# List scheduling carried on through the last two chunks, the routing, the first weight split and the gathering

## The chip, the cores and the metric

One core of one Trainium2 chip. The metric is device time in microseconds (us) of one execution of the whole program. The engines are TensorE (PE, matmuls; PEld its weight loads), VectorE (DVE), ScalarE (ACT), GpSimd (POOL) and SyncE (SP, which here only starts DMAs). Each engine works through its own list of instructions in order.

## The reference

A recurrence over 768 steps for 4 batches x 8 heads with a 40x40 state, and then a mixture of experts on its 3072 output rows (320 wide, 8 experts, inner width 1024):

```python
for t in range(S):
    y[:, :, t] = einsum('bhd,bhde->bhe', r[:, :, t], state)
    Sa = einsum('bhde,bhe->bhd', state, a[:, :, t])
    state = state*w[:, :, t][:, :, None, :] - einsum('bhd,bhe->bhde', Sa, b[:, :, t])
    state = state + einsum('bhd,bhe->bhde', v[:, :, t], k[:, :, t])
x = y.transpose(0, 2, 1, 3).reshape(3072, 320)
do_compute = x @ w_skip > 0; xc = x[do_compute]; logits = xc @ w_gate
out = x; out[do_compute] = xc + softmax(logits).max(1) * (relu(xc @ w1[e]) @ w2[e])   # e = argmax(logits)
```

## The kernel before

**The recurrence** runs in NC=24 chunks of 32 steps, in 6 phases of 4 chunks. The 32 (batch, head) pairs are handled in two halves w=0 and w=1. Decays and triangular systems (32x32 inverses, on DVE) are prepared per pair of chunks and for the next phase; they depend on the inputs alone. What depends on the chunk before is a chain, which runs once for each chunk c and half w:

- `rs` (PE `pc<-rrt,SS`, odd chunks' end): the decayed state goes into the operand tile R1;
- `ux` (PE `pc<-R1t,L1t`, then one ACT copy to UX), `uq` (PE `pc<-UX,TB`, then four ACT copies `R1t<-pc`);
- two mask multiplies on the corner of R1 (`R1t<-R1t,mc 64x256`, POOL; DVE in chunk 23);
- `sst` (PE `ps<-R1t,L2t`, two groups, 104 columns in an even chunk, 72 in an odd one, 32 in the last): from its result ACT (even chunks) or DVE (odd chunks) copies the state into the R1 of the next chunk, and DVE forms YT, the chunk's output, transposed;
- in odd chunks `pc<-L2t,R1t`, whose copy SS feeds the next `rs`.

When both halves of a chunk are done, `yt` (PE `pc<-mc,YT`) turns YT round, the rows go to XS and by DMA to out, and `pq<-wx,YT` gives the scores. `route` picks each token's expert: DVE, a small rank matmul `pq<-oh,mc` on PE, more DVE, and an indirect DMA `xg<-XS,ix` that POOL starts and that collects the rows of each expert in memory. In the table below a chunk is bounded by the start of its DMA `out<-XS`.

**The end.** The rows of the first expert are loaded ahead (`ex`), and the tokens of the last two chunks are added by one-hot matmuls: `xacc` (`pc<-mc,ex`) and two `xadd` (`pc<-ex,XS`, for chunks 22 and 23). Meanwhile split(0) has turned the first expert's raw weights WR into a rounded top part WH and a rest WL = WR - WH, each 128x5632. Then `l1` of expert 0 begins (`px<-xH,WH`); all eight experts follow, and out rows are written by scatter DMAs.

**What sets the order.** Class Rec records instructions as tasks with their reads and writes. plan() is a list scheduler with a table of costs per engine (cost()), a priority (keys(): place in the program less the length of the path behind it), and the PSUM banks: want() gives a task that opens a new tile a bank of its group when it starts, PC+PQ (`pc_101` to `pc_103`, `pq_100`) or PS (`ps_104`, `ps_105`); `px_106` and `px_107` are given by hand. flush() then emits each engine's instructions in the order of the planned starts. What is recorded appears in the profile as L255, what is emitted directly, in the order of the program text, as L129. In this kernel the recording ends ahead of chunk 22:

```python
if c==22:
    with tc.manual_schedule(engines={ET.Pool}): rec.flush()
    ...
    tg=m.split(0)
```

The storage of WH and WL of expert 0 is that of M, scratch of the inverses, which is given free there. Calls written out by hand (`T()` takes one step of split(0), `RP` one of the routing) place the rest in chunks 22 and 23. `warm(k)` is a 128x512 matmul on constants with no reader; it is emitted only while nothing is recorded, so here at WT[0] and WT[4].

Of the kernel before, what the change touches and what calls it, by code (L numbers as in the profile page):

```python
# [1097 lines left out]
```

## Time and profile before

| | us |
|---|---|
| three runs | 650.41, 658.1, 656.82 (median 656.82) |
| profiled execution, its own time | 658.57 |
| its span, first to last instruction | 656.8 |
| mean granted TensorE clock | 0.858 |
| PE, DVE, ACT, POOL busy | 500.1, 489.9, 370.5, 283.8 |
| start to first `out<-XS` (chunk 0 out) | 118.87 |
| from there to `out<-XS` of chunk 18, at 436.49 | 317.62 |
| from there to `rs` of chunk 22, at 468.00 | 31.51 |
| `rs` of chunk 22 to the first matmul of expert 0 | 55.54 |
| experts | 133.26 |

Busy time of one engine counts instructions of that engine alone; "[1.34 <-POOL R1t]" behind an instruction is the idle time of its engine ahead of it and the instruction that ended that idle time. PEclk is the granted TensorE clock as a share of 2.4 GHz (0.5 is 1.2 GHz). The start times are counted from the start of the span.

### The profile page before, as it was taken

To read this page: it belongs to the slowest core of one execution; us is meant where nothing else is said; L and a number is where in the kernel's file an instruction comes from. 1 tells how busy PE (TensorE), PEld (TensorE's weight loads), DVE (VectorE), ACT (ScalarE), POOL (GpSimd) and SP (SyncE) were. 2 spreads that over 40 slices of the span, in tenths; PEclk is the share of its full clock that TensorE was granted. 3 is DMA by queue.
4 is the path that set the end of the run, shared out by engine and by line. 5 is a ranking of instruction groups with operands and counts; after the bars stand their busy time and mean duration, and the time that the engine had idled before them with its cause. 6 is when DMAs were issued, how large, how long until landed. Compare 5 with 4: busy or idle time off the path is not lost. (4 is left out here: it accounts for less than half of the span.)

```text
span 656.8 us, 25441 instructions
## 1 busy us (share of the span) xinstructions
PE 500.1 (76%) x10688; PEld 439.2 (67%) x10688; DVE 489.9 (75%) x1367; ACT 370.5 (56%) x890; POOL 283.8 (43%) x214
## 2 busy tenths in 40 slices
PE   0354368878787876867878978787766999999995
PEld 0343357766676766756767867676655599999995
DVE  8974849977986798696899777983672357888871
ACT  6244247765775766655885675775353055554440
POOL 5560244544545555236454532221311156666661
PEclk9999557878886898869896896887886699999999
DMA  7755762434542325234442535453242067776110
GB/s 218 203 142 140 213 202 44 121 103 113 158 128 71 113 82 155 74 98 118 132 126 82 144 78 127 133 170 108 59 130 73 21 187 227 225 223 212 52 49 24
DMA packets 74801, 83.34 MB, mean 127 GB/s; under 512 B 33598, under 2 KB 52619, under 8 KB 74680
## 3 DMA queue, kind: packets, MB, share of 16 engines
q1 hardware_dynamic: 72760, 77.85, 41.6%
q0 software_dynamic: 1920, 3.79, 1.6%
q8 instruction: 86, 1.41, 0.9%
q14 instruction: 35, 0.29, 0.1%
HBM read 70.75 MB, written 13.15 MB: 128 GB/s over the span
## 5 line engine op out<-in xcount | busy, mean ns | idle before, releaser
L255 POOL TENSOR_TENSOR R1t<-R1t,mc 64x256 f32<-64x256 f32 x86 | 67.9, 789 | 129.7 <-ACT R1t L255 66.8
L255 ACT COPY R1t<-pc 32x416 f32<-32x416 f32 (+3 forms) x251 | 95.6, 381 | 41.8 <-PE pc L255 35.4
L255 PE MATMUL ps<-R1t,L2t 128*40 128x104 f32 (+1 forms) x1376 | 84.3, 286 | 10.4 <-DVE YT L255 4.7
L255 PEld LDWEIGHTS ps<-R1t,L2t 128*40 128x40 f32 x1376 | 71.6, 143 | 18.2 <-issue 12.1
L255 DVE TENSOR_TENSOR px<-px,M 128x48 f32<-128x48 f32 (+24 forms) x240 | 59.8, 266 | 2.5
L129 POOL TENSOR_TENSOR WL<-WR,WH 128x1280 fp32r<-128x1280 f32 (+1 forms) x21 | 57.9, 2790 | 8.1 <-ACT WH L129 8.0
L255 POOL TENSOR_TENSOR WR<-WR,M 104x1024 f32<-104x1024 f32 x19 | 42.6, 2249 | 42.5 <-DVE M L255 21.6
L255 DVE TENSOR_TENSOR M<-M,px 128x48 f32<-128x48 f32 (+26 forms) x240 | 56.3, 253 | 2.7 <-ACT px L255 0.6
L255 ACT COPY R1t<-ps 40x288 f32<-40x288 f32 x88 | 34.6, 394 | 20.0 <-PE ps L255 18.3
L129 ACT CAST WH<-WR 128x1024 fp32r<-128x1024 f32 (+1 forms) x35 | 39.6, 1132 | 0.0
L255 DVE TENSOR_TENSOR R1t<-ps,D 40x160 f32<-40x160 f32 x84 | 26.9, 320 | 16.8 <-PE ps L255 14.6
L255 DVE TENSOR_TENSOR_SCAN M<-M 104x1041 f32<-104x1041 f32 (+1 forms) x15 | 39.0, 2597 | 0.1
L255 ACT COPY L2t<-pc 64x160 f32<-64x160 f32 x108 | 31.0, 287 | 13.5 <-PE pc L255 11.3
L255 PE MATMUL pc<-UX,TB 32*32 32x104 f32 (+1 forms) x1152 | 35.1, 267 | 3.6 <-issue 1.9
L129 DVE CAST ti<-xe 128x2 int32<-128x2 f32 x8 | 37.1, 4632 | 0.2
L129 POOL DMA_INDIRECT out<-ro,ti x16 | 16.2, 1013 | 46.4 <-DVE hL L129 12.5
L129 ACT ACTIVATE hH<-pc 128x512 fp32r<-128x512 f32 x21 | 12.6, 598 | 38.8 <-PE pc L129 32.9
L255 POOL DMA_INDIRECT xg<-XS,ix x20 | 20.3, 1017 | 28.7 <-DVE ix L255 7.5
L129 PE MATMUL pc<-xH,WH 128*128 128x256 f32 x126 | 32.5, 283 | 0.2 <-DVE hL L129 0.2
L255 PEld LDWEIGHTS pc<-UX,TB 32*32 32x32 f32 x1152 | 26.8, 121 | 8.1 <-issue 3.4
L129 DVE TENSOR_TENSOR WL<-WR,WH 128x1024 fp32r<-128x1024 f32 (+1 forms) x19 | 24.2, 1272 | 10.2 <-ACT WH L129 9.7
L255 PE MATMUL pc<-mc,WR 104*128 104x104 f32 x140 | 23.8, 310 | 8.2 <-ACT R1t L255 4.6
(285 smaller groups left out, 1410.1 us busy)
## 6 DMA issues: line engine op xcount, KB each, us to landing
WR<-w SPq DMA_DIRECT2D x16, 640.0 KB
WR<-kb SPq DMA_DIRECT2D x48, 208.0 KB
WR<-w SPq DMA_DIRECT2D x16, 512.0 KB
vvt<-vv SPq DMA_DIRECT2D x24, 208.0 KB
rrt<-rr SPq DMA_DIRECT2D x24, 208.0 KB
SCR<-vv SPq DMA_DIRECT2D x22, 208.0 KB
...
```

The costliest lines, as they stand in the source:

```text
L129: if not s.on: return fn(*a,**k)
L255: for fn,a,k,own in s.tasks[i].calls: (fn if s.en[i]==s.tasks[i].e else s.nc.vector.tensor_copy)(*[at(x,own) for x in a],**{n:at(x,own) fo ...
```

## The change

1. Recording goes on to the end of the recurrence's function: chunks 22 and 23, the routing, split(0), `ex`, `xacc` and `xadd` are tasks too, and flush() comes behind them. M's storage is handed over within the recording (home, swap, gone): the first write to WH waits for all earlier uses of M.
2. split(0) is cut into 11 pieces of 512 columns. In the plan a WH copy may go to DVE or ACT, a WL subtraction to DVE or POOL, and the masks of chunks 22 and 23 to DVE or POOL, by costs of their own (t.w). The penalty for taking an engine other than the task's own is 0.3 instead of 1.0 from chunk 21 on (ALT2).
3. The cost of a PE row in the plan is lower (a transpose .0925 for .144, and so on), and PE tasks that write `px` get a path of 10 us behind them (END).
4. A matmul group that accumulates claims its whole bank. In want(), when one bank of a group is free, only the oldest tile of that group that has none may take it.
5. The tiles into which the gathering adds are `px_107` and a PS bank instead of two `pc` banks. The two `warm` matmuls are not emitted, since recording is on.

```diff
+        if n==s.home and s.gone==1: s.gone=2; return [(('s',n),15,(1<<13400)-1)]
...
-            if op=='transpose': return 0.144,0.2
-            return (0.0019*m if m>64 else 0.064 if m>40 else 0.008+0.00077*o if m==40 else 0.02 if m<32 else max(0.024,0.007+0.00034*o)),0.2
+            if op=='transpose': return 0.0925,0.2
+            return (0.01+0.00167*o if m>64 else max(0.057,0.008+0.00083*o) if m>40 else 0.003+0.00084*o if m>32 else max(0.0185,0.001+0.00042*o)),0.2
...
+        if e=='P' and k.get('start') is not k.get('stop'): W=[(n,15,(1<<512)-1) for n,q,f in W]
...
+        t.w={}
+        if t.v: t.w['V']=t.v
+        if s.flex:
+            n=int(np.prod([d[1] for d in w[0].ap[1:]]))
+            t.w=dict(A=0.17+0.00095*n,V=0.08+0.0006*n) if op in ('copy','tensor_copy') else dict(V=0.08+0.00107*n,G=0.2+0.0021*n)
+            t.d=t.w.pop(e)
...
-            t.up=t.d*s.PW+max([s.tasks[j].up+t.lat+t.x+(s.HOP if s.tasks[j].e!=t.e else 0) for j in t.n],default=0)
+            t.up=t.d*s.PW+max([s.tasks[j].up+t.lat+t.x+(s.HOP if s.tasks[j].e!=t.e else 0) for j in t.n],default=s.END if t.e=='P' and t.out[0]=='px' else 0)
...
-            while old and old[0] in bank: old.pop(0)
             for o in T[i].al:
                 if o in bank: continue
                 av=[(at[k],k) for k in at if at[k] is not None and k not in got.values() and (k in s.rest)==(s.first[o] in s.rest)]
                 if not av: return None
+                g=s.first[o] in s.rest; q=old[g]
+                while q and q[0] in bank: q.pop(0)
+                if len(av)==1 and q[0]!=o: return None
...
-                if best is None or x[0]+(s.ALT if e!=T[x[1]].e else 0)<best[0]+(s.ALT if best[3]!=T[best[1]].e else 0): best=x+(e,)
+                alt=lambda y,f: y[0]+((s.ALT if y[1]<s.late else s.ALT2) if f!=T[y[1]].e else 0)
+                if best is None or alt(x,e)<alt(best,best[3]): best=x+(e,)
...
-    LET=1.0; FAR=1.0; ALT=1.0; FILL=None
+    END=10.0; ALT2=0.3; late=1e9; LET=1.0; FAR=1.0; ALT=1.0; FILL=None
...
-WT=(1,0,0,0,1)
+WT=(1,0,0,0,1); LATE=22
...
-        L=c==NC-1
+        L=c>NC-3; rec.flex=L
...
             (V if L else G).tensor_tensor(o,o,mQ[r].unsqueeze(1).broadcast_to([64,8,32]),ALU.mult)
+        rec.flex=0
...
-            if c==20: m.load(0)
-            if c==22:
-                with tc.manual_schedule(engines={ET.Pool}): rec.flush()
-                mp.__exit__(None,None,None)
-                wp=m.ctx.enter_context(tc.tile_pool(name="mwa",bufs=1,side="right")); m.WA=[wp.tile([128,5632],F32,name=n) for n in ("WH0","WL0")]; ex=wp.tile([128,1408],F32,name="ex")
-                tg=m.split(0)
+            if c==LATE-2: m.load(0)
+            if c==21: rec.late=len(rec.tasks)
+            if c==LATE: rec.gone=1; tg=m.split(0)
...
-        p2=[m.pr[0].tile([128,512],F32) for _ in range(2)]; pt=[p2[0][:,0:256],p2[0][:,256:512],p2[1][:,0:256]]
+        pz=ps_s.tile([128,256],F32); po=rec.own[pz.name]; pt=[PX[1][:,0:256],PX[1][:,256:512],pz]
...
-        warm(WT[4]); m.xadd(pt,xl[:,1],1); m.pt0=pt; m.p2=p2
+        warm(WT[4]); m.xadd(pt,xl[:,1],1)
+        with tc.manual_schedule(engines={ET.Pool}): rec.flush()
+        m.pt0=pt[:2]+[rec.banks[rec.bank_of[po]][:,0:256]]
...
-        cut=[(0,1024,V,128),(1024,2048,V,128),(2048,3072,G,128),(3072,4352,G,128),(4352,5632,G,128)]
+        cut=[(0,1024,V,128),(1024,2048,V,128),(2048,3072,G,128),(3072,4352,G,128),(4352,5632,G,128)] if e else [(q,q+512,V,128) for q in range(0,5632,512)]
         for a,b,E,pe in cut:
-            s.top(A if e else V,h[:,a:b],r[:,a:b])
-            if e==0: yield
-            s.low(E if e else V,l[:pe,a:b],r[:pe,a:b],h[:pe,a:b]); yield
+            s.rec.flex=s.rec.on; s.top(A if e else V,h[:,a:b],r[:,a:b])
+            s.low(E if e else V,l[:pe,a:b],r[:pe,a:b],h[:pe,a:b]); s.rec.flex=0; yield
```

The plan as a whole is another one; the order of all recorded chunks differs too. Three places follow; names with a number are tiles or PSUM banks, `UX_141` and `UX_142` belong to half 0 and half 1, SS_119 and SS_120 likewise.

PE in chunks 22 and 23. Before, from `rs` of chunk 22, half 1 (`ps` rows of 104 columns belong to chunk 22, of 32 to chunk 23):

```order
L129 MATMUL pc_102<-UX_141,TB 32x104 x16
L129 MATMUL pc_103<-rrt_124,SS_120 40x64 x16
L129 MATMUL ps_104<-R1t,L2t 40x104 x8
L129 MATMUL ps_105<-R1t,L2t 40x104 x8
L129 MATMUL pc_101<-R1t,L1t 32x104 x16
L129 MATMUL pq_100<-rrt_124,SCR 64x32 x8
L129 MATMUL pq_100<-oh_150,mc 32x16 x8
L129 MATMUL pc_102<-UX_142,TB 32x104 x16
L129 MATMUL pc_103<-R1t,L1t 32x72 x16
L129 MATMUL ps_104<-R1t,L2t 40x104 x8
L129 MATMUL ps_105<-R1t,L2t 40x104 x8
L129 MATMUL pc_101<-mc,YT_121 128x104 x4
```

Now, from `uq` of chunk 22, half 0:

```order
L273 MATMUL pc_102<-UX_141,TB 32x104 x16
L273 MATMUL pc_101<-rrt_124,SCR 64x32 x8
L273 MATMUL pc_103<-R1t,L1t 32x104 x16
L273 MATMUL pq_100<-rrt_124,SCR 64x32 x8
L273 MATMUL pc_102<-oh_150,mc 32x16 x8
L273 MATMUL pc_103<-UX_142,TB 32x104 x16
L273 MATMUL ps_104<-R1t,L2t 40x104 x8
L273 MATMUL ps_105<-R1t,L2t 40x104 x8
L273 MATMUL pc_103<-R1t,L1t 32x72 x16
L273 MATMUL pc_102<-UX_141,TB 32x72 x16
L273 MATMUL ps_105<-R1t,L2t 40x104 x8
L273 MATMUL ps_104<-R1t,L2t 40x104 x8
```

`uq` of half 1 stood behind `sst` of half 0 and stands ahead of it now; `uq` of chunk 23, half 0 (`UX_141`, 72 columns) stood behind `sst` of chunk 22, half 1, and `yt`, and stands ahead of them now.

PE at the end, from the last `sst` to the first matmul of expert 0. Before:

```order
L129 MATMUL ps_105<-R1t,L2t 40x32 x8
L129 MATMUL ps_104<-mc 128x512
L129 MATMUL pc_102<-mc,YT_122 128x104 x4
L129 MATMUL pq_100<-wx,YT_122 64x9 x8
L129 MATMUL pc_101<-mc,ex 128x128 x2
...
L129 MATMUL pc_102<-ex,XS_145 64x256 x2
L129 MATMUL pq_100<-oh_150,mc 32x8 x8
L129 MATMUL ps_104<-mc 128x512
L129 MATMUL pc_101<-ex,XS_145 128x256 x2
L129 MATMUL pc_102<-ex,XS_145 64x256 x2
L129 MATMUL px_106<-xH,WH_7262 128x256
```

Now:

```order
L273 MATMUL ps_105<-R1t,L2t 40x32 x8
L273 MATMUL pc_103<-wx,YT_122 64x9 x8
L273 MATMUL pc_102<-mc,YT_122 128x104 x4
L273 MATMUL px_107<-mc,ex 128x128 x2
...
L273 MATMUL ps_105<-mc,ex 64x128 x2
L273 MATMUL pc_102<-oh_150,mc 32x8 x8
L273 MATMUL px_107<-ex,XS_145 128x256 x2
L273 MATMUL ps_105<-ex,XS_145 64x256 x2
L273 MATMUL px_107<-ex,XS_145 128x256 x2
L273 MATMUL ps_105<-ex,XS_145 64x256 x2
L130 MATMUL pc_101<-xH,WH_6943 128x256
```

The two 128x512 matmuls are gone, the scores of chunk 23 come ahead of its `yt`, and its rank matmul comes ahead of the first `xadd`.

POOL around chunk 22, now (before, POOL had no piece of split(0); six masks in a row stood here, with the last four `xg` DMAs behind them):

```order
L273 TENSOR_TENSOR WL_6944<-WR,WH_6943 128x512
L273 TENSOR_TENSOR R1t<-R1t,mc 64x8x32
L273 DMA xg<-XS_145,ix_155 2048x322
L273 TENSOR_TENSOR R1t<-R1t,mc 64x8x32 x2
L273 TENSOR_TENSOR WL_6944<-WR,WH_6943 128x512 x4
L273 TENSOR_TENSOR R1t<-R1t,mc 64x8x32
L273 DMA xg<-XS_144,ix_154 2048x322 x2
```

Six WL pieces stand in POOL's list, four of them ahead of the one mask of chunks 22 and 23 that is left on POOL; the other seven masks, two WH copies and five WL pieces are on DVE, nine WH copies on ACT. (Before: five of each, in larger pieces, all on DVE.)

PE at the start, before, from the fourth row of its list (`kbt` is `mc,WR`; `WR 32x64`, `WR,M` and `WR,L1t` give the triangular systems, `M 16x16` and `TB,SCR` the end of the first inverse):

```order
L255 MATMUL pc_101<-mc,WR 128x104 x4
L255 MATMUL pc_101<-WR 32x64 x64
L255 MATMUL pc_101<-WR,M 32x64 x64
L255 MATMUL pc_101<-rrt_123,vvt 64x64 x8
...
L255 MATMUL pc_101<-rrt_124,vvt 64x64 x8
L255 MATMUL pq_100<-M 16x16 x32
L255 MATMUL pc_103<-M 16x16 x32
L255 MATMUL pq_100<-TB,SCR 16x16 x32
```

Now:

```order
L273 MATMUL pc_101<-WR 32x64 x64
L273 MATMUL pc_101<-mc,WR 128x104 x16
L273 MATMUL pc_101<-WR,M 32x64 x64
L273 MATMUL pc_101<-rrt_123,vvt 64x64 x16
L273 MATMUL pc_101<-R1t,WR 32x104 x32
L273 MATMUL pc_101<-rrt_123,rrt_124 64x32 x16
L273 MATMUL pc_101<-WR,L1t 32x64 x64
L273 MATMUL pc_101<-M 16x16 x32
L273 MATMUL pc_101<-TB,SCR 16x16 x32
L273 MATMUL pc_101<-UX_141,TB 32x104 x16
```

All four `kbt` of the first pair now come ahead of the second group of systems (`WR,M`), and the matmuls that end the inverse use `pc_101` instead of waiting for `pq_100` and `pc_103`.

## Rows read from the trace of the kernel before

**Rows 1.** Busy time of each engine by stage (from:to, length, then busy us and instructions of PE, weight loads, DVE, ACT, POOL; granted TensorE clock; DMA share; GB/s). The first row is from the start of `out<-XS` of chunk 2 to that of chunk 6, and so on by four chunks to chunk 18; then the stages are cut at `rs` of chunk 22, `uq` of chunk 22, the last `sst`'s end and the first matmul of expert 0.

```profile
161.69:234.31 72.62, 57.65 (x1504) 48.93 (x1500) 58.94 (x204) 47.85 (x127) 37.58 (x30) 0.83 0.38 108
234.31:305.30 70.99, 55.23 (x1397) 47.41 (x1392) 58.40 (x203) 48.74 (x130) 34.82 (x30) 0.81 0.38 108
305.30:370.56 65.26, 52.54 (x1435) 44.94 (x1426) 55.19 (x204) 45.27 (x119) 35.16 (x29) 0.85 0.41 118
370.56:436.49 65.93, 55.00 (x1427) 46.84 (x1424) 53.20 (x215) 45.11 (x119) 17.04 (x22) 0.87 0.45 121
436.49:468.00 31.51, 25.32 (x608) 21.34 (x603) 14.28 (x50) 19.18 (x51) 7.80 (x10) 0.84 0.38 108
468.00:479.40 11.40, 8.27 (x201) 6.97 (x197) 9.59 (x19) 3.34 (x8) 2.84 (x2) 0.85 0.35 93
479.40:509.73 30.33, 19.56 (x456) 16.17 (x452) 15.50 (x54) 14.26 (x38) 5.48 (x6) 0.74 0.33 101
509.73:523.54 13.81, 13.49 (x72) 7.86 (x73) 3.33 (x22) 1.06 (x4) 1.44 (x2) 0.58 0.06 18
```

**Rows 2.** PE's instructions in chunks 22 and 23, in order of time: start, length, instruction, idle time ahead of it and what ended it.

```profile
468.01 1.09 PE L129 MATMUL pc<-rrt,SS 40*40 40x64 f32 x32
...
479.40 0.92 PE L129 MATMUL pc<-UX,TB 32*32 32x104 f32 x32
...
484.03 3.00 PE L129 MATMUL ps<-R1t,L2t 128*40 128x104 f32 x30 [0.42 <-POOL R1t L129]
...
490.02 0.92 PE L129 MATMUL pc<-UX,TB 32*32 32x104 f32 x32
490.86 0.71 PE L129 MATMUL pc<-R1t,L1t 128*32 128x72 f32 x32
...
493.88 2.90 PE L129 MATMUL ps<-R1t,L2t 128*40 128x104 f32 x30 [0.65 <-POOL R1t L129]
...
499.07 0.70 PE L129 MATMUL pc<-UX,TB 32*32 32x72 f32 x32
...
508.44 1.28 PE L129 MATMUL ps<-R1t,L2t 128*40 128x32 f32 x30 [0.47 <-DVE R1t L129]
```

**Rows 3.** What PE waited for from 468 to 524 us: engine and tile waited for, us in total, times, longest.

```profile
PE ps L129 <- POOL R1t L129: 6.0, 6, 1.9
```

**Rows 4.** POOL's and then DVE's instructions in chunk 22, in order of time.

```profile
470.68 2.92 POOL L129 TENSOR_TENSOR R1t<-R1t,mc 64x256 f32<-64x256 f32 x2 [7.53 <-ACT R1t L129]
...
492.08 0.72 POOL L129 TENSOR_TENSOR R1t<-R1t,mc 64x256 f32<-64x256 f32 x1 [8.10 <-ACT R1t L129]
...
471.38 1.63 DVE L129 TENSOR_TENSOR WL<-WR,WH 128x1024 fp32r<-128x1024 f32 x1
```

**Rows 5.** Groups of one shape, over the whole span: count, busy us, mean ns of one, idle time before.

```profile
L255 ACT COPY R1t<-pc 32x416 f32<-32x416 f32 x69 | 34.3, 497 | 19.8 <-PE pc L255 18.5 <-DVE R1t L255 0.4
L255 ACT COPY R1t<-pc 32x288 f32<-32x288 f32 x67 | 26.1, 390 | 10.3 <-PE pc L255 8.2 <-PE ps L255 1.1
L255 ACT COPY R1t<-ps 40x288 f32<-40x288 f32 x88 | 34.6, 394 | 20.0 <-PE ps L255 18.3 <-issue 0.3 <-PE pc L255 0.2
L255 ACT COPY UX<-pc 128x288 f32<-128x288 f32 x18 | 7.2, 399 | 8.1 <-PE pc L255 7.7 <-ACT L2t L255 0.2
L255 POOL TENSOR_TENSOR R1t<-R1t,mc 64x256 f32<-64x256 f32 x86 | 67.9, 789 | 129.7 <-ACT R1t L255 66.8 <-PE pc L255 26.7 <-DMA xg<-XS,ix 13.1
L129 DVE TENSOR_TENSOR R1t<-R1t,mc 64x256 f32<-64x256 f32 x4 | 1.7, 420 | 4.3 <-ACT R1t L129 4.3
L129 DVE TENSOR_TENSOR WL<-WR,WH 128x1024 fp32r<-128x1024 f32 x17 | 21.2, 1247 | 10.1 <-ACT WH L129 9.7
L129 POOL TENSOR_TENSOR WL<-WR,WH 128x1280 fp32r<-128x1280 f32 x14 | 41.3, 2973 | 0.0
```

**Rows 6.** PE from the last `sst` to expert 0, in order of time.

```profile
510.05 2.07 PE L129 MATMUL ps<-mc 128*128 128x512 f32 x2 [0.34 <-DVE YT L129]
511.92 0.90 PE L129 MATMUL pc<-mc,YT 104*128 104x104 f32 x4
512.75 1.03 PE L129 MATMUL pq<-wx,YT 104*64 104x9 f32 x16
513.71 3.63 PE L129 MATMUL pc<-mc,ex 128*128 128x128 f32 x16
517.27 3.12 PE L129 MATMUL pc<-ex,XS 128*128 128x256 f32 x8
520.32 0.40 PE L129 MATMUL pq<-oh,mc 128*32 128x8 f32 x16
520.65 1.44 PE L129 MATMUL ps<-mc 128*128 128x512 f32 x2
521.93 1.61 PE L129 MATMUL pc<-ex,XS 128*128 128x256 f32 x8
```

**Rows 7.** The table of rows 1 for 5 us of that and for `l1` of expert 0, columns as there.

```profile
510.00:515.00 5.00, 4.95 (x28) 3.31 (x30) 1.19 (x8) 0.64 (x2) 0.97 (x1) 0.50 0.07 20
...
523.54:533.00 9.46, 9.25 (x71) 8.53 (x72) 5.76 (x9) 5.44 (x9) 1.50 (x2) 1.00 0.53 153
```

**Rows 8.** PE in the opening, in order of time.

```profile
52.85 0.96 PE L255 MATMUL pc<-mc,WR 104*128 104x104 f32 x4 [1.27 <-ACT L2t L255]
...
80.24 0.73 PE L255 MATMUL pq<-M 32*16 32x16 f32 x63 [8.06 <-ACT L2t L255]
...
89.27 1.60 PE L255 MATMUL pq<-UX,TB 32*32 32x104 f32 x31
```

More of the change, by code (lines that the diff above doesn't have):

```diff
@@ L44 @@
 class Task:
-    __slots__=("e","op","calls","R","W","d","lat","out","p","n","pr","al","up","k","v","x","g")
+    __slots__=("e","op","calls","R","W","d","lat","out","p","n","pr","al","up","k","v","x","g","w")
 class Eng:
@@ L67, in __init__ @@
     def __init__(s,nc):
-        s.nc=nc; s.on=False; s.ni=0; s.tasks=[]; s.own={}; s.na=0; s.first={}; s.cache={}; s.banks={}; s.rest=()
+        s.nc=nc; s.on=False; s.ni=0; s.tasks=[]; s.own={}; s.na=0; s.first={}; s.cache={}; s.banks={}; s.rest=(); s.home=None; s.flex=0; s.gone=0; s.new=None
         n=s.shim=Shim(); n.nc=nc
@@ L135, in call @@
         r=[y for x in list(a[1:])+[v for n,v in k.items() if n!='accum_out'] for y in ap(x)]
-        W=[u for x in w for u in s.use(x)]; R=[u for x in r for u in s.use(x)]
+        W=[u for x in w for u in s.use(x)]
+        if e=='P' and k.get('start') is not k.get('stop'): W=[(n,15,(1<<512)-1) for n,q,f in W]
+        R=[u for x in r for u in s.use(x)]
         d,lat=s.cost(e,op,w,r,a)
-        own=dict(s.own)
+        own=dict(s.own); own[None]=s.gone
         L=s.tasks[-1] if s.tasks else None
@@ L177, in put @@
             pool[T[i].e].append(i)
-            if T[i].v and not keep and s.ALT<9: pool['V'].append(i)
+            if not keep and s.ALT<9:
+                for f in T[i].w: pool[f].append(i)
         for i in range(N):
@@ L194, in plan @@
         pos=s.POS0; blk=0; got=0.0; dq=0.0; track=[(0,0.0)]
-        done=0; old=sorted(users); lv=lg=0.0
+        done=0; old=[[o for o in sorted(users) if (s.first[o] in s.rest)==g] for g in (False,True)]; lv=lg=0.0
         while done<N:
@@ L205, in plan @@
                 c.sort(key=lambda x:s.key[x[1]])
-                x=c[0]; du=lambda i: T[i].v if e!=T[i].e else T[i].d
+                x=c[0]; du=lambda i: T[i].w[e] if e!=T[i].e else T[i].d
                 while True:
@@ L215, in plan @@
                 bank[o]=k; at[k]=None
-            en[i]=e; st[i]=t0; fin[i]=t0+(t.v if e!=t.e else t.d)
+            en[i]=e; st[i]=t0; fin[i]=t0+(t.w[e] if e!=t.e else t.d)
             if e=='P':
@@ L248, in at @@
         def at(x,own):
+            if isinstance(x,bass.AP) and x.name==s.home and own[None]:
+                s.new=s.new or s.swap()
+                p,f=divmod(x.offset,x.ap[0][0]); o,t=max(((o,t) for o,t in s.new if o<=f),key=lambda y:y[0])
+                st=t.ap[0][0]; y=bass.AP(t.tensor,t.offset+p*st+f-o,[(st,x.ap[0][1])]+[tuple(d) for d in x.ap[1:]])
+                return y if x.dtype==F32 else y.bitcast(x.dtype)
             if isinstance(x,bass.AP) and x.name in s.banks:
@@ L254, in flush @@
             if isinstance(i,tuple): s.FILL(*i); continue
-            for fn,a,k,own in s.tasks[i].calls: (fn if s.en[i]==s.tasks[i].e else s.nc.vector.tensor_copy)(*[at(x,own) for x in a],**{n:at(x,own) for n,x in k.items()})
+            for fn,a,k,own in s.tasks[i].calls: (fn if s.en[i]==s.tasks[i].e else s.nc.scalar.copy if s.en[i]=='A' else s.nc.vector.tensor_copy if 'copy' in s.tasks[i].op else s.nc.gpsimd.tensor_tensor)(*[at(x,own) for x in a],**{n:at(x,own) for n,x in k.items()})
         s.tasks=[]
@@ L304, in attn, with swap @@
     WR=m.WR
-    mp=tc.tile_pool(name="M",bufs=1,side="right"); M=mp.__enter__().tile([128,13272],F32,name="M")
+    mp=tc.tile_pool(name="M",bufs=1,side="right"); M=mp.__enter__().tile([128,13272],F32,name="M"); m.WA=[M[:,0:5632],M[:,5632:11264]]; ex=M[:,11264:12672]
+    def swap():
+        mp.__exit__(None,None,None)
+        wp=m.ctx.enter_context(tc.tile_pool(name="mwa",bufs=1,side="right")); m.WA=[wp.tile([128,5632],F32,name=n) for n in ("WH0","WL0")]; m.WH[0],m.WL[0]=m.WA
+        return [(0,m.WA[0]),(5632,m.WA[1]),(11264,wp.tile([128,1408],F32,name="ex"))]
+    rec.home,rec.swap=M.name,swap
     off=[0]
```

## The prediction

> **What bounds the kernel now.** I read the table by stage first, for where no engine is full; then PE's instructions in time order in the stage that stands out, with what PE waited for there; then POOL and DVE in the same stretch; last the opening.
>
> The four middle stages of four chunks are bounded by no single engine [rows 1]: PE is busy 78 to 83% of them, DVE 81 to 85%, and work of the same kind took 72.62 us in one and 65.93 in another. From 161.69 to 436.49 that is 274.8 us for 16 chunks, 17.2 a chunk. The reader should see that spread: an order of instructions alone is worth 7 us in four chunks.
>
> The end is worse. Chunks 22 and 23 from `rs` to the first matmul of expert 0 take 11.40 + 30.33 + 13.81 = 55.54 us [rows 1], with PE busy 19.56 of the 30.33 and a clock of 0.74 there and 0.58 behind it. The order explains it [rows 2]: `uq` of chunk 22 starts at 479.40 for half 0 and only at 490.02 for half 1, 10.6 us later, behind the whole of `sst` of half 0. Half 0 has all that its chunk 23 needs at about 488 (its second `sst` matmuls end at 484.03 + 3.00 = 487.03, two copies of 0.39 follow [rows 5]), but its `uq` of chunk 23 starts at 499.07. The halves run one behind the other, and each leaves PE idle at its masks: PE waited 6.0 us for POOL's [rows 3]. In chunk 22 the pair of masks took 2.92 us on POOL beside the weight split on DVE, and 0.72 each without it [rows 4].
>
> Behind the last `sst` PE is full, at clock 0.50 [rows 7], and does `yt`, the scores, the gathering and two constant matmul bursts [rows 6].
>
> **The change, part by part.**
>
> *To `uq` of chunk 22.* DVE's share of split(0) leaves this stretch and `rs` of half 0 stands farther ahead. Of 11.40 us PE was busy 8.27 [rows 1], so at most 3.1 us can go, and `pq<-rrt,SCR` (0.6 us) now stands behind. Ends: 0 and -3.8. I take **-3**, nearer the upper end, since the masks' excess alone is 2.92 - 2 x 0.72 = 1.5.
>
> *`uq` of chunk 22 to the last `sst`.* One half's chain, from rows: `uq` 0.92 [rows 2], four copies at 0.50 = 2.0 [rows 5], a mask 0.79 [rows 5], `sst` 3.0 [rows 2], two copies at 0.39 = 0.8, `ux` 0.71 [rows 2], the UX copy 0.40, `uq` 0.70 [rows 2], four copies at 0.39 = 1.6 [rows 5], a mask 0.42 on DVE [rows 5], `sst` 1.28 [rows 2]: 12.6 us, and some 0.2 for each of ten handovers would make it 14.6. Half 1 now starts behind two small products and one `ux`, an estimate of 4 us: 18.6. PE's own work is 19.56 us at clock 0.74; at the 0.83 of the middle stages and their 80% busy share it is 17.4/0.80 = 21.8. I take 22, since PE's load decides then: **-8.3**. Ends: -12 (the chains alone) and -3 (half of the overlap lost to handovers).
>
> *The tail.* The bursts of 2.07 and 1.44 us [rows 6] go. The first is ahead of `yt` while PE has nothing else; the second fills the wait for DVE behind the rank matmul. That matmul (0.40) stood behind the first `xadd` and now runs ahead of it, so DVE's share of the routing is done when the second `xadd` comes. What is left is 0.90 + 1.03 + 3.63 + 3.12 + 0.40 + 1.61 = 10.7 us, most of it at the half level. All at the full level it would be near 6 to 7 (the two `xadd`, equal work, took 3.12 and 1.61). Ends: -1 (still half) and -7. Middle: **-4**.
>
> *split(0) elsewhere.* Its DVE work, five copies and five subtractions of 0.7 to 1.6 us [rows 4, 5], some 11 us, now lies in chunks 20 to 22, spread over ACT, DVE and POOL in pieces of 512 columns. Cover: in the 31.5 us ahead of `rs` of chunk 22 DVE is busy 14.28, ACT 19.18 and POOL 7.80 [rows 1]. POOL is the risk: a piece, by the 1280-column row of 2.97 us [rows 5], takes 1.2, and six stand in its list, four of them directly ahead of the mask of chunk 22. Ends 0 and +5; I take **+1**.
>
> The Trainium skill speaks against these POOL pieces (page "SBUF — State Buffer", section "SBUF: two separate sides"): DVE with two SBUF operands and GpSimd take a shared port pair in turn, each for a whole instruction. The 2.92 us for two masks beside the split [rows 4] agree; no row before shows a short WL piece on POOL.
>
> *The opening.* `uq` of chunk 0 starts at 89.27; 8.06 us ahead of that PE waits at 80.24 for a bank, which ACT empties [rows 8]. By the bank rule that work runs in `pc_101`, so the wait can go. But three `kbt` (0.96 each with a wait of 1.27 [rows 8]) move ahead of `WR,M`, on which the first inverse rests: up to 3 x 2.23 = 6.7 us on the other side. Most of it comes back, since the same `kbt` no longer stand between that inverse's other matmuls, as the one at 52.85 did [rows 8]. Ends -8 and +6.7; I take **-5**.
>
> *The middle.* Re-planned with other PE costs and the bank rule. Nothing in the rows says which way: **0**, ends -13 (the two slow stages down to 65.5) and +16 (all at 18.2 a chunk).
>
> *Expert 0.* `l1` takes 9.46 us at clock 1.00 [rows 7], behind the second burst. Without it the full level may come later. Ends 0 and +9.3; I take **+1**, since the two `xadd` still run back to back ahead of it.
>
> The Trainium skill speaks against leaving the bursts out (page "TensorE: Matmul & The Clock Gate", section "Part 1: The HAM clock gate"): the throttled level is the default and work releases it. The clock of 0.50 at 510 to 515 [rows 7], behind a stage in which PE waited a third of the time, agrees; by the rule `l1` would stand at half level if PE pauses ahead of it.
>
> **Sum:** -3 - 8.3 - 4 + 1 - 5 + 0 + 1 = -18.3. The profiled execution took 658.57, so 640.3; that execution lies 1.75 above the median of the three runs, 656.82, and from the median it is 638.5. I say **639**.
>
> **Rivals.**
>
> 1. *Only the end gains.* The opening gives nothing and `l1` starts at half level for half its length (+5): -15.3 + 1 + 5 = -9, so 648 (645 to 656). For it: `kbt` ahead of `WR,M`, and the clock of 0.50. Against: the wait of 8.06 us is real. Chance 0.20.
> 2. *The middle gains too.* The stages of 72.62 and 70.99 us come down to the 65.5 of the others: a further -12.6, so 627 (620 to 632). For it: a better bank rule where all wait a little. Against: the old plan already found 65.3 in two of four, and a new one can lose those. Chance 0.15.
> 3. *The middle loses: slower.* The plan counts PE rows at the full clock, while 0.81 to 0.87 was granted [rows 1]. PE then runs behind the plan, and engines that keep a fixed order wait at the instructions planned too early. The place is every chunk from 2 to 18; the gain of 18.3 is eaten at 18.3/16 = 1.1 us a chunk more than 17.2, that is from 18.3, and at 18.9 it is 666. Against: it changes an order, no duration, and the old costs were no closer for all shapes. Chance 0.09 (657 to 676).
> 4. *The end is not as planned.* POOL's four WL pieces come late and hold the mask of chunk 22 by 5 us, and PE stays at half level through the overlap, where its 19.56 us would grow toward 26: last stages 50 us instead of 40, so 650 (646 to 657). Chance 0.08.
>
> **How the numbers follow.** The forecast (632 to 645) has 0.48. About 2% of the median, 13 us, is what runs of this kernel, which lie 7.7 us apart, can tell from no change: below 643.7 is faster, above 670 slower. Faster: most of the forecast (0.44), rival 2 (0.15) and a little of rival 1: 0.60. Slower: half of rival 3 and a little for mishaps: 0.06. The rest, 0.34, is within. The range of 8 in 10 takes in rivals 1 and 4 nearly whole and half of rival 2: 624 to 657.
>
> **What would show it.** In the changed kernel's trace: from `rs` of chunk 22 to `l1` 38 to 42 us instead of 55.5; the two `uq` of chunk 22 within 5 us; `sst` of the halves alternating with no wait over 1 us for a mask; the clock in that stretch at 0.8 or more. `uq` of chunk 0 at 80 to 85 instead of 89.27, and the first `out<-XS` some 5 us ahead of 118.87. 17.2 us a chunk in the middle. The forecast is wrong if the middle moves by over 0.5 us a chunk, if POOL's WL pieces end behind the copies that its mask waits for, or if `l1` of expert 0 takes over 12 us.

## The result, and the profile after

The changed kernel takes 629.17 us (median of 4 runs, 624.97 to 633.08) beside 654.04 before (4 runs, 650.41 to 658.1): ratio 0.9617, 95% interval 0.9522 to 0.9713, faster. Two profiled executions make the sum: 658.57 (span 656.8) before, 630.49 (span 628.7) after, 28.1 us less. The profiled execution before was longer than all four of its runs, 4.5 us above their median, at a granted clock of 0.858 (0.903 after), so some of the 28.1 belongs to it and not to the change.

The table by stage of the changed kernel (columns as in [rows 1]); the cuts are the start of the first `out<-XS`, then of those of chunks 2, 6, 10, 14 and 18, `rs` and `uq` of chunk 22, the end of the last `sst`, the first matmul of expert 0:

```profile
0.00:110.08 110.08, 50.16 (x1454) 42.23 (x1456) 74.76 (x137) 52.35 (x126) 48.70 (x31) 0.96 0.60 171
110.08:150.86 40.78, 35.02 (x976) 29.96 (x976) 38.22 (x138) 28.78 (x78) 21.25 (x18) 0.82 0.36 103
150.86:215.25 64.39, 49.11 (x1419) 42.71 (x1410) 56.49 (x204) 45.11 (x120) 30.00 (x27) 0.89 0.44 125
215.25:281.41 66.16, 52.82 (x1472) 44.76 (x1470) 59.84 (x217) 45.96 (x121) 37.20 (x28) 0.87 0.44 126
281.41:358.34 76.93, 62.82 (x1648) 54.10 (x1647) 63.82 (x219) 50.76 (x134) 38.82 (x33) 0.80 0.37 104
358.34:417.99 59.65, 47.97 (x1347) 40.84 (x1344) 48.23 (x199) 41.85 (x111) 20.49 (x23) 0.91 0.44 119
417.99:453.11 35.12, 30.26 (x782) 25.12 (x781) 25.89 (x78) 23.41 (x62) 11.49 (x14) 0.90 0.50 146
453.11:461.61 8.50, 6.91 (x189) 5.92 (x185) 6.53 (x19) 5.37 (x13) 5.74 (x6) 1.00 0.55 136
461.61:484.95 23.34, 16.77 (x439) 13.82 (x438) 15.34 (x58) 11.99 (x31) 3.46 (x5) 0.82 0.38 104
484.95:493.86 8.91, 8.57 (x68) 5.93 (x67) 3.10 (x19) 0.96 (x4) 1.89 (x2) 0.72 0.10 30
493.86:628.70 134.84, 123.99 (x940) 121.76 (x940) 96.32 (x110) 60.65 (x82) 74.00 (x37) 0.98 0.48 146
```

The three stages of 55.54 us in [rows 1] take 8.50 + 23.34 + 8.91 = 40.75 now. The opening is 110.08 for 118.87. Between them lie 343.03 us for 349.14. The experts take 134.84 for 133.26. So -14.8, -8.8, -6.1 and +1.6. The 343.03 are 307.91 up to the `out<-XS` of chunk 18 (317.62 before) and 35.12 from there to `rs` of chunk 22 (31.51 before).

PE in chunks 22 and 23 of the changed kernel, in time order, beside [rows 2]:

```profile
461.61 0.92 PE L273 MATMUL pc<-UX,TB 32*32 32x104 f32 x32
...
467.34 1.61 PE L273 MATMUL pc<-UX,TB 32*32 32x104 f32 x32 [0.81 <-DVE UX L273]
468.88 3.00 PE L273 MATMUL ps<-R1t,L2t 128*40 128x104 f32 x32
...
474.81 0.70 PE L273 MATMUL pc<-UX,TB 32*32 32x72 f32 x32 [1.25 <-ACT UX L273]
475.44 1.63 PE L273 MATMUL ps<-R1t,L2t 128*40 128x104 f32 x32
...
480.61 0.70 PE L273 MATMUL pc<-UX,TB 32*32 32x72 f32 x32
```

The `uq` of chunk 22 are 5.7 us apart instead of 10.6, and half 0's `uq` of chunk 23 comes 13.2 us behind its `uq` of chunk 22 instead of 19.7. PE's waits for the masks, which are the waits of `sst` (`ps`) for R1, shrink as well. Before, DVE's masks of chunk 23 cost 3.5 us beside the 6.0 of POOL's in [rows 3]; now there are 1.6 and 0.5 (first row 468 to 524 us before, the others 453 to 494 us after):

```profile
PE ps L129 <- DVE R1t L129: 3.5, 4, 1.4
...
PE ps L273 <- POOL R1t L273: 1.6, 2, 1.1
...
PE ps L273 <- DVE R1t L273: 0.5, 1, 0.5
```

The tail, beside [rows 6] (`px<-mc,ex` and `px<-ex,XS` are the 128-partition parts of `xacc` and `xadd`):

```profile
486.28 0.95 PE L273 MATMUL pc<-mc,YT 104*128 104x104 f32 x4
487.03 1.10 PE L273 MATMUL px<-mc,ex 128*128 128x128 f32 x4
...
490.26 0.31 PE L273 MATMUL pc<-oh,mc 128*32 128x8 f32 x16
490.50 1.13 PE L273 MATMUL px<-ex,XS 128*128 128x256 f32 x4
...
493.86 0.38 PE L130 MATMUL pc<-xH,WH 128*128 128x256 f32 x1
```

Both `xadd` stand behind the rank matmul. `xacc` (487.03 to 490.3) is little faster than its 3.63 us before, but the first `xadd` (490.50 to 492.2) takes 1.7 for 3.12. That is the clock of this execution and not the order: in another trace of the same kernel (632.94 us, below) the first `xadd` took 3.0 again, 490.82 to 493.86, and the tail 11.4 us at clock 0.55:

```profile
490.49 0.40 PE L273 MATMUL pc<-oh,mc 128*32 128x8 f32 x16
490.82 2.08 PE L273 MATMUL px<-ex,XS 128*128 128x256 f32 x4
492.83 1.12 PE L273 MATMUL ps<-ex,XS 128*64 128x256 f32 x4
```

The opening, beside [rows 8] (the first row is of the kernel before, the others of the changed one):

```profile
35.39 1.93 PE L255 MATMUL pc<-WR,M 40*32 40x64 f32 x64 [1.19 <-DVE M L255]
...
44.84 1.93 PE L273 MATMUL pc<-WR,M 40*32 40x64 f32 x64 [1.27 <-ACT L2t L273]
...
76.18 0.74 PE L273 MATMUL pc<-M 32*16 32x16 f32 x64 [3.93 <-DVE M L273]
77.42 0.74 PE L273 MATMUL pc<-TB,SCR 16*16 16x16 f32 x64 [0.51 <-ACT TB L273]
79.52 1.61 PE L273 MATMUL pc<-UX,TB 32*32 32x104 f32 x32 [1.36 <-DVE TB L273]
```

`WR,M` comes at 44.84, 9.5 us later than before (35.39), but the wait of 8.06 us for a bank is a wait of 3.93 for DVE's inverse, and `uq` of chunk 0 starts at 79.52, not 89.27.

### The profile page after: what moved, and what is told of

The parts are those of the page before. It is cut to its first block, busy times and chain, and to the rows that moved or that the text cites. A ratio compares the mean times of both kernels' runs of the same rounds, so it can differ in the third digit from the quotient of the medians.

```text
span 628.7 us, 25427 instructions
## 1 busy us (share of the span) xinstructions
PE 484.4 (77%) x10684; PEld 427.1 (68%) x10684; DVE 488.5 (78%) x1390; ACT 367.2 (58%) x876; POOL 293.1 (47%) x217
## 4 chain that ended last, share of the span: by engine, by line
PE 39%; DVE 34%; issue 9%; DMA 7%; ACT 7%; POOL 1%; SPq 0%; POOLq 0%; DVEq 0%; ACTq 0%
PE pc L273 16%; DVE M L273 9%; PE ps L273 8%; DVE R1t L273 7%; DVE px L273 6%; PE pc L130 4%; PE pq L273 4%; PE ps L130 3%; ACT R1t L273 3%; PE px L130 3%; DVE WR L273 2%; DVE ti L130 2%; DMA out<-ro,ti 2%; DMA xe<-xg 2%; DVE YT L273 1%
## 5 line engine op out<-in xcount | busy, mean ns | idle before, releaser
L273 ACT COPY R1t<-pc 32x288 f32<-32x288 f32 (+3 forms) x290 | 110.4, 381 | 41.6 <-PE pc L273 32.6
L273 PE MATMUL ps<-R1t,L2t 128*40 128x104 f32 (+2 forms) x1536 | 92.3, 278 | 16.5 <-issue 6.3
L273 PEld LDWEIGHTS ps<-R1t,L2t 128*40 128x40 f32 x1536 | 77.6, 139 | 25.3 <-issue 16.9
L273 DVE TENSOR_TENSOR M<-M,px 128x48 f32<-128x48 f32 (+22 forms) x240 | 57.1, 253 | 3.8 <-ACT px L273 1.5
L273 POOL DMA_INDIRECT xg<-XS,ix x24 | 27.5, 1146 | 52.6 <-DVE YT L273 16.6
L273 PE MATMUL pc<-UX,TB 32*32 32x72 f32 (+1 forms) x1280 | 39.0, 266 | 12.3 <-ACT R1t L273 2.9
L273 PEld LDWEIGHTS pc<-UX,TB 32*32 32x32 f32 x1280 | 29.5, 121 | 18.1 <-ACT R1t L273 4.2
L130 POOL DMA_INDIRECT out<-ro,ti x16 | 16.2, 1011 | 48.1 <-DVE ro L130 10.6
L130 ACT ACTIVATE hH<-pc 128x512 fp32r<-128x512 f32 x22 | 13.2, 598 | 42.2 <-PE pc L130 42.2
L273 DVE TENSOR_TENSOR_SCAN M<-M 104x1041 f32<-104x1041 f32 (+1 forms) x15 | 36.0, 2401 | 0.2
L273 DVE TENSOR_TENSOR R1t<-ps,D 40x160 f32<-40x160 f32 x88 | 28.1, 320 | 9.4 <-PE ps L273 8.4
L273 ACT COPY L2t<-pc 64x160 f32<-64x160 f32 x95 | 27.2, 287 | 12.5 <-PE pc L273 9.7
L273 PE MATMUL pq<-mc,WR 104*128 104x104 f32 x60 | 10.8, 316 | 26.2 <-POOL WR L273 24.7
```

Of the source, the lines that this page charges most:

```text
L130: if not s.on: return fn(*a,**k)
L273: for fn,a,k,own in s.tasks[i].calls: (fn if s.en[i]==s.tasks[i].e else s.nc.scalar.copy if s.en[i]=='A' else s.nc.vector.tensor_copy if ' ...
```

## The experiments

The change has parts that can be taken alone. Three questions: which part pays in which stage; why the middle moved; what the clock has to do with it. In the table "opening" is the start to the first `out<-XS`, "middle" goes from there to the first `rs` of chunk 22, "end" from there to the first matmul of expert 0; times in us of the profiled execution. Lines of one letter ran on one chip, beside the kernel before (medians 652.0, 654.6 and 653.4 for a, b and c). The two kernels traced twice with the same plan show what an execution alone is worth: the changed one gave 343.0 and 344.2 in the middle and 40.8 and 44.6 at the end (clock there 0.83 and 0.73), the recording alone 325.6 and 327.3, and 34.9 and 34.3. The kernel before and its variant without bursts, which have the same order up to chunk 22, gave 349.1 and 344.7 in the middle.

| | kernel | median | opening | middle (clock) | end |
|---|---|---|---|---|---|
| | before | 654.0 | 118.9 | 349.1 (0.84) | 55.5 |
| | changed | 629.2 | 110.1 | 343.0 (0.86) | 40.8 |
| a | recording only | 616.4 | 117.8 | 325.6 (0.91) | 34.9 |
| a | rules and new costs only | 641.0 | 110.0 | 336.3 (0.89) | 57.1 |
| a | changed, old costs | 630.5 | 104.8 | 354.3 (0.85) | 34.9 |
| a | before, no bursts | 655.8 | 120.1 | 344.7 (0.85) | 54.3 |
| b | recording only, PW 1.27 | 627.4 | 116.2 | 338.8 (0.85) | 37.2 |
| b | recording only, rule in chunks 0, 1 | 616.9 | 103.7 | 337.0 (0.88) | 35.2 |
| b | changed, fillers | 620.5 | 108.6 | 336.2 (0.91) | 40.3 |
| b | changed, no split on POOL | 621.1 | 108.6 | 340.0 (0.87) | 39.4 |
| c | changed again | 628.7 | 107.6 | 344.2 (0.85) | 44.6 |
| c | recording only again | 616.5 | 119.2 | 327.3 (0.90) | 34.3 |
| c | recording only, fillers | 614.7 | 118.8 | 330.1 (0.90) | 31.6 |
| c | changed, fillers again | 621.8 | 109.6 | 334.9 (0.90) | 41.0 |

**Recording alone.** The costs are the old ones, and the bank rule and the whole-bank claim are gone. Parts 1, 2 and 5 of the change stay, and of part 3 the path of 10 us behind `px`:

```diff
+            if op=='transpose': return 0.144,0.2
+            return (0.0019*m if m>64 else 0.064 if m>40 else 0.008+0.00077*o if m==40 else 0.02 if m<32 else max(0.024,0.007+0.00034*o)),0.2
...
-        if e=='P' and k.get('start') is not k.get('stop'): W=[(n,15,(1<<512)-1) for n,q,f in W]
...
-                if len(av)==1 and q[0]!=o: return None
```

> The changed kernel with the old PE costs, without the bank rule and without the whole-bank claim: only the recording of the end (with the cut of the split and the free choice of engines) is left. Theory A (each part pays in its own stage): rs of chunk 22 to expert 0 about 41 us as in the changed kernel (40.8), first out near 119 as before (118.9), the middle near that of before; total about 642. Theory B (the bank rule and the new costs carry the gain everywhere, the recording alone little): the last stage over 48 us and the total 650 or more.

Its stages (opening; middle; from `rs` to 466.00; the rest of the end; experts):

```profile
0.00:117.76 117.76, 50.88 (x1572) 43.59 (x1572) 87.70 (x158) 57.29 (x140) 46.04 (x34) 0.99 0.59 164
117.76:443.32 325.56, 263.23 (x7520) 224.62 (x7520) 288.74 (x1035) 235.46 (x619) 160.80 (x140) 0.91 0.45 127
443.32:466.00 22.68, 18.39 (x573) 15.16 (x568) 16.11 (x62) 15.06 (x38) 4.51 (x6) 1.00 0.42 104
466.00:478.26 12.26, 10.77 (x96) 7.45 (x90) 3.66 (x22) 0.95 (x4) 1.94 (x2) 0.58 0.31 88
478.26:611.00 132.74, 123.90 (x941) 121.67 (x940) 94.98 (x110) 60.63 (x82) 73.47 (x37) 0.98 0.47 145
```

616.40 us, ratio 0.9503 (0.9411 to 0.9595), below both theories. Opening as before and a short end: theory A there. But the middle, which A had left as it was, is 23.6 us shorter, with the rules and costs of the kernel before (19.1 us shorter than its other trace, 344.7).

**The rules and the new costs alone**, in the kernel before, with chunk 22 onward in the order of the program:

```diff
-            if op=='transpose': return 0.144,0.2
+            if op=='transpose': return 0.0925,0.2
...
+        if e=='P' and k.get('start') is not k.get('stop'): W=[(n,15,(1<<512)-1) for n,q,f in W]
...
-            while old and old[0] in bank: old.pop(0)
+                if len(av)==1 and q[0]!=o: return None
```

> The kernel before with the new PE costs, the bank rule and the whole-bank claim, the recording still ending ahead of chunk 22. Theory A: first out near 110 as in the changed kernel, rs of chunk 22 to expert 0 near 55 as before; total 641 to 648, by how the middle falls out. Theory B: 636 or less.

640.95 us, ratio 0.989 (0.9781 to 0.9999), as A has it: opening 110.0, end 57.1. The clock in its end is low as well (first row, `rs` to 491.00, 0.63, where [rows 1] have 0.85 and then 0.74):

```profile
446.31:491.00 44.69, 31.88 (x652) 26.19 (x648) 25.18 (x69) 17.55 (x46) 8.00 (x8) 0.63 0.31 92
491.00:503.42 12.42, 12.04 (x75) 6.96 (x73) 3.42 (x22) 1.06 (x4) 1.44 (x2) 0.69 0.07 22
```

**The old costs in the changed kernel:**

```diff
-            if op=='transpose': return 0.0925,0.2
+            if op=='transpose': return 0.144,0.2
```

> The changed kernel with the old PE costs alone. Theory A: the opening has the same order and takes the same time (first out near 110), the last stage about 41 us, the middle 340 to 350; total 628 to 637, so the costs are worth little in themselves. Theory C (the costs are what brings the middle and the end forward): total over 640.

630.50 us, ratio 0.9686 (0.9557 to 0.9814): the costs are worth nothing in the total, as A said. The stages differ, though: opening 104.8, end 34.9, and the longest middle of all, so that A's reading of the opening ("the same order") was wrong behind the first 13 rows of PE's list:

```profile
0.00:104.79 104.79, 46.02 (x1396) 39.74 (x1398) 73.39 (x121) 50.01 (x119) 45.07 (x30) 1.00 0.62 174
104.79:459.11 354.32, 286.23 (x7672) 243.90 (x7668) 298.03 (x1064) 238.84 (x632) 162.57 (x141) 0.85 0.41 117
```

This plan and the recording alone differ by the bank rule (the whole-bank claim moves only the last matmuls of the gathering): opening -13.0, middle +28.8. Whether the rule costs that, or the plan had luck, is the next pair.

**One number of the planner that has nothing to do with it:**

```diff
-    HOP=0.08; PW=1.25; FETCH=4.0;
+    HOP=0.08; PW=1.27; FETCH=4.0;
```

> The recording-only kernel with one number of the planner changed that has nothing to do with the change (weight of a task's own length in the priority, PW, 1.27 for 1.25), which gives another order of the middle. Theory D (the middle is the luck of the plan): its middle, first out to rs of chunk 22, moves away from 325.6 us, towards the 337 to 354 of the other plans; total 620 to 640. Theory E (the longer recording itself makes the middle faster): the middle stays within 320 to 331 and the total within 611 to 622.

627.35 us, ratio 0.9513 (0.9413 to 0.9613); the middle is 338.8, 13.2 longer than with 1.25, and the clock 0.85:

```profile
116.21:455.01 338.80, 278.16 (x7488) 237.78 (x7489) 287.85 (x1033) 232.35 (x613) 164.01 (x138) 0.85 0.43 120
```

Theory D: what the middle takes is the luck of the plan. The two plans, with nearly the same count of matmuls, also tell what differs: PE is idle 60.6 us here and 62.3 there, but busy 278.2 instead of 263.2. The end stays short (37.2).

**The rule for chunks 0 and 1 alone:**

```diff
-                if len(av)==1 and q[0]!=o: return None
+                if i<s.late0 and len(av)==1 and q[0]!=o: return None
...
+            if c==2: rec.late0=len(rec.tasks)
```

> The recording-only kernel with the bank rule for the tasks of chunks 0 and 1 alone. First out by the rule near 105 to 110 instead of 117.8 under every theory. Theory E with F (the rule itself costs time in the middle, as old costs with rule 354.3 against 325.6 without): the middle stays near 326 and the total is 603 to 610. Theory D: the middle lands anywhere between 325 and 354, total 605 to 635.

616.85 us, but its four executions spread from 607.83 to 626.01, too wide to set it above or below the recording alone; the two lowest, 607.83 and 610.65 (the traced one), are the shortest times of all runs here. The opening is 103.7, 14 us shorter than without the rule; the middle 337.0, without a rule in it. So the rule pays in the opening, and by the way that was forecast: PE's wait ahead of `M 16x16`, for ACT's copies, is 8.05 to 8.08 us in every plan without the rule, and 3.7 to 3.9, for DVE's inverse, in every plan with it; the first `uq` starts at 89.3 to 91.5 us without it and at 78.7 to 80.1 with it. That the rule costs time in the middle (theory F) is not shown: most plans lie at 335 to 345 with it or without.

**Why plans differ in the middle.** From 325.6 to 354.3 us PE's idle time is nearly the same, 62.3 us in the shortest and 68.1 in the longest (stretch less busy time); PE's busy time goes from 263 to 286 (with 2% more matmuls, 7672 for 7520, which the shorter opening leaves over), and the clock from 0.91 to 0.85. A place in the slow stage of the changed kernel (columns as in [rows 1]), and two `sst` in it:

```profile
288.00:292.00 4.00, 3.46 (x162) 2.96 (x160) 3.91 (x5) 2.84 (x10) 1.60 (x2) 1.00 0.48 148
292.00:296.00 4.00, 2.45 (x92) 2.07 (x83) 1.26 (x5) 0.90 (x2) 1.82 (x3) 0.93 0.58 167
296.00:300.00 4.00, 4.00 (x81) 3.59 (x78) 3.23 (x12) 2.63 (x7) 4.00 (x3) 0.65 0.28 77
...
312.00:316.00 4.00, 3.00 (x53) 2.68 (x53) 2.46 (x10) 3.36 (x10) 1.49 (x1) 0.50 0.53 171
...
303.44 1.63 PE L273 MATMUL ps<-R1t,L2t 128*40 128x104 f32 x32
...
314.56 2.98 PE L273 MATMUL ps<-R1t,L2t 128*40 128x104 f32 x32
```

PE is busy 2.45 us of four, and in the next four, where it is full, the granted clock has fallen to a mean of 0.65. The two `sst` are equal work: the one at the full level took 1.63 us, the one at 0.50 (the half level) 2.98. That the clock is what makes PE's busy time longer is so far argued. To try it I filled pauses that the plan shows from chunk 1 on with matmuls on constants, whose result nobody reads:

```diff
+            if c==1: nf=[0]; rec.FILL=lambda t,n: nf.__setitem__(0,nf[0]+1) or (nf[0]>20 and m.tc.nc.tensor.matmul(t[:,0:n],m.tri,m.mc[:,0:n],start=True,stop=True))
```

> The changed kernel with some 30 matmuls on constants, which nobody reads, of 110 to 512 columns put into PE's planned pauses from chunk 1 on. Theory G (the middle's length goes with the granted clock, 0.84 to 0.91 over the plans, which pauses of PE let fall): clock of the middle above its 0.86, middle shorter than 343 by 5 to 15 us though PE does some 12 us more, total 615 to 625. Rival: the fillers stand in real work's way or change nothing: middle 343 or longer, total 629 to 640.

Middle of the kernel with fillers, then the share of its 24 fillers (48 records; PE busy, weight loads, clock); 7 more lie in the end:

```profile
108.57:444.80 336.23, 277.13 (x7650) 231.51 (x7646) 292.57 (x1052) 236.36 (x626) 160.10 (x139) 0.91 0.43 122
108.57:444.80 336.23, 18.37 (x48) 8.35 (x48) 0.91 0.43 122
```

620.47 us, ratio 0.9486 (0.9430 to 0.9541). The fillers take 18.4 us of PE and the real work 277.1 - 18.4 = 258.8 instead of 278.0; the middle is 6.8 us shorter. Theory G holds for the middle. The total says nothing yet, since the changed kernel had run on another chip, and on this one it took 621.13 without fillers and without POOL's pieces (below); so the pair was repeated on one chip:

> The changed kernel itself, beside the three below on one chip. It gives 621 to 632; first out 108 to 111, middle 338 to 345, rs of chunk 22 to expert 0 39 to 42 under every theory (same order).

> The changed kernel with the fillers again, now beside the changed kernel. Theory G: clock of the middle higher by 0.03 to 0.05 than in the changed kernel, middle 4 to 10 us shorter, total 4 to 10 us less. Rival: within 3 us of the changed kernel, since what the clock gives the fillers take.

628.70 (621.83 to 632.94, 6 runs; ratio to before 0.9698, 0.9613 to 0.9783) without, 621.83 (618.15 to 626.22; 0.9619, 0.9536 to 0.9701) with them: 6.9 us less by medians, some 1%, though the two intervals overlap. The traced execution of the changed kernel was the longest of its six (632.94), with an end of 44.6 us where 39 to 42 was expected; beside it the middle with fillers is 9.3 us shorter (344.2 to 334.9), and the real work of PE 260.7 instead of 280.1. And where the clock was high already:

> The recording-only kernel again (old costs, no bank rule). Theory D2 (its lead over the change is a better middle and a shorter end of this plan, not of the chip): 612 to 621, 8 to 14 us below the changed kernel on the same chip, with a middle of 324 to 331. Rival (the lead was the execution's): within 5 us of the changed kernel.

> The recording-only kernel with 22 matmuls on constants in PE's planned pauses from chunk 1 on. Theory G (clock): its middle already has the clock 0.91, so little is left to win: within 5 us of the recording-only kernel, 610 to 622. Rival (fillers help by another way than the clock): 6 us or more below it.

616.47 (ratio 0.953, 0.9451 to 0.9609) and 614.72 (0.9501, 0.9421 to 0.9582): the lead of the recording alone repeats, 12.2 us below the change on one chip, and fillers add 1.8 by medians, as theory G has it. Its trace shows where: the 12 fillers of the middle left its clock at 0.90 and the middle 2.8 us longer, and those of the end brought the clock there from 0.85 to 1.00 and took 2.7 off it. The last is the fastest kernel here by its median, some 14 us below the change; it and the recording alone can't be told apart.

**The bursts**, left out of the kernel before:

```diff
-WT=(1,0,0,0,1)
+WT=(0,0,0,0,0)
```

> The kernel before without its two 128x512 constant bursts. Theory A (they only cost their time): the tail of 13.8 us falls by 2 to 3.5 us and l1 of expert 0 keeps 9.5 us; total 651 to 653. Rival (they hold the clock up for expert 0): the tail falls, but l1 begins at the half level and takes 12 us or more; total 654 to 660.

The tail, from the last `sst`, falls from 13.81 to 11.41, and `l1` still starts at the full level (first matmul to the last ahead of `l2`):

```profile
507.70:519.11 11.41, 9.81 (x69) 6.50 (x69) 3.31 (x22) 1.06 (x4) 1.44 (x2) 0.67 0.07 22
519.11:529.47 10.36, 9.47 (x71) 8.32 (x71) 6.45 (x10) 6.33 (x9) 2.40 (x2) 1.00 0.52 167
```

The trace goes with theory A in the tail; but `l1` takes 10.36 us for 9.2, and the time is 655.76 for 651.98, ratio 1.0079 (1.0041 to 1.0118): no gain, and outside A's 651 to 653. The rival's total (654 to 660) came, but not its reason, since the clock of `l1` was 1.00. Why it isn't faster stays open.

**No split on POOL:**

```diff
-else dict(V=0.08+0.00107*n,G=0.2+0.0021*n)
+else dict(V=0.08+0.00107*n) if n>256 else dict(V=0.08+0.00107*n,G=0.2+0.0021*n)
```

> The changed kernel with no piece of the first split on POOL (all subtractions on DVE, copies still on ACT or DVE); same order up to chunk 19. Theory A (the split is covered wherever it lies): rs of chunk 22 to expert 0 within 1.5 us of 40.8, total within 3 us of 629. Rival (DVE, which carries copies and masks there, is the limit): the stretch from chunk 20's out to expert 0 longer by 3 to 6 us. Rival (POOL's pieces and DVE's stand in each other's way): shorter by 2 to 4 us.

The end is 39.36 us, 1.4 less: theory A within its bound, and less than two executions of the changed kernel differ by (40.8 and 44.6). The stretch named in the rivals, from the `out<-XS` of chunk 20, is 39.1 for 44.8, but that bound has moved itself: `rs` of chunk 22 stands 4.05 us behind it in the changed kernel and 0.23 ahead of it here. From the `out<-XS` of chunk 18 it is 74.66 for 75.87. So no run shows POOL's pieces to be a bottleneck of the changed kernel, though one of DVE's met them:

```profile
457.27 5.03 POOL L273 TENSOR_TENSOR WL<-WR,WH 128x512 fp32r<-128x512 f32 x4
...
452.74 0.69 DVE L273 TENSOR_TENSOR WL<-WR,WH 128x512 fp32r<-128x512 f32 x1
460.65 2.20 DVE L273 TENSOR_TENSOR WL<-WR,WH 128x512 fp32r<-128x512 f32 x1
```

A piece of the same size took 0.69 us alone and 2.20 beside POOL. The median of this kernel, 621.13, lies 8 us below the changed kernel's, more than A's bound; only 1.4 of it is in the stage that differs, and the two weren't run on one chip, so the rest isn't attributed.

## Why the prediction was right, and what was off

Forecast 639 in a range of 624 to 657; measured 629.17, faster, as said. The time lies outside the narrower 632 to 645 that the forecast had to itself, and in the 620 to 632 of rival 2 (the middle gains too), which had a chance of 0.15. The mechanisms of the end and the opening were right; that the time was lower than forecast came mostly from the middle, for which the prediction had no reason either way. By its own steps:

- *To `uq` of chunk 22*: -3 forecast, 11.40 to 8.50 measured, -2.9. Right in this execution; in the other trace of the changed kernel it took 11.68, at clock 0.76. The pair of masks of 2.92 us, which feeds the last `sst` of chunk 21 and not one of chunk 22, takes 1.52 now, as expected.
- *To the last `sst`*: -8.3 forecast, 30.33 to 23.34, -7.0. Right in kind: the halves overlap. That PE's load then decides is not shown: PE was busy 16.77 of the 23.34, 72% where 80% was set, and waited 5.2 us for DVE and 1.2 for ACT. The other trace shows 21.49. All traces of plans that record the end show 31.6 to 44.6 us for the whole of it, those that don't 54.3 to 57.1: this part of the gain is shown by the runs, its size only to some us.
- *The tail*: -4 forecast, 13.81 to 8.91, -4.9. Its clock rose from 0.58 to 0.72, which was luck: with the same order and a clock of 0.55 it took 11.43, -2.4, as much as leaving out the bursts alone gave (13.81 to 11.41). The recording alone had a tail of 12.26 at 0.58. `l1` started at the full level (9.21 us at clock 1.00; 9.20 before, the 9.46 being the length of the window in [rows 7]), so the +1 set for it wasn't due there; the experts as a whole took 1.6 longer in this execution, and 131.7 to 135.1 over all of them, which no run explains. The Trainium skill's rule (page "TensorE: Matmul & The Clock Gate", section "Part 1: The HAM clock gate (the "warmup" mystery)") that the lower level is the default, held against leaving out the bursts, did not decide here: `l1` started at the full level behind the two `xadd`. In the middle the traces agree with it: 0.65 behind a pause, and 0.91 for 0.86 with fillers.
- *split(0)*: +1 forecast, +3.6 measured. The stage from the `out<-XS` of chunk 18 to `rs` of chunk 22 is 35.12 for 31.51; with no piece on POOL 35.3 (413.38 to 448.68), so POOL isn't what lengthened it; what did stays open, with DVE busy 25.89 us in it for 14.28. A POOL piece took 5.03/4 = 1.26, the estimate was 1.2. The 2.20 us of DVE's piece agree with what the Trainium skill says of the shared port pair (page "SBUF — State Buffer", section "SBUF: two separate sides"). No other DVE piece of that trace took over 0.69.
- *The opening*: -5 forecast, -8.8 measured. The mechanism was right: with the rule 103.7 to 110.1, without it 116.2 to 120.1, whatever else is changed. Mis-sized was the loss by the `kbt` moved ahead, which came back wholly: `WR,M` starts 9.5 us later, and yet the first `uq` 9.75 earlier.
- *The middle*: 0 forecast with ends of -13 and +16. With split(0) taken apart it is the stretch up to chunk 18, 317.62 to 307.91, -9.7. This is the term that carries most of the error of 10 us, and part of it is the execution: the same order took 313.17 in the kernel without bursts. By the prediction's own sign of being wrong, 0.5 us a chunk, it came to the edge: 16.70 a chunk from chunk 2 on for 17.18. "Nothing in the rows says which way" was right, and the bounds held for this plan; the recording alone, at -23.6 for the whole middle, falls outside them. Rival 2 was right about the two slow stages, which came down to 64.39 and 66.16, but the third rose from 65.26 to 76.93 and the fourth fell to 59.65, so its reason was only half of it. What I missed is what most of the spread between plans goes with: not PE's idle time but its busy time and the granted clock, which the rows already showed beside the stages, 0.83 and 0.81 in the slow, 0.85 and 0.87 in the fast ones [rows 1]. Between the kernel before and the changed one it is otherwise: PE is busy 279.0 and 278.0 us in the middle, and the idle time fell from 70.1 to 65.0.
- *Rival 3*, that counting PE at the full clock spoils the middle, has no run for it: with the old costs the middle is longer, 354.3 for 343.0, and one irrelevant number moves it by 13.
- *Rival 4* did not come: POOL's four pieces ended at 462.30, 2.26 us ahead of the mask behind them, and PE ran at 0.82 in the overlap, and at 0.81 in the other trace. Its price was set too low, for at the half level 19.56 us at 0.74 would be 29 and not 26.

So of 28.1 us between the two profiles the recording of the end brings 14.8 (10.9 by the other trace of the changed kernel) and the bank rule 8.8 in the opening; the 6.1 of the middle are the luck of this plan and of the executions as far as the runs tell (0.5 to 6.1 over the traces of either order), and can't be put down to a part of the change.
